# A chunked linear-attention kernel: transpositions of the decays traced at the end of a group's preparation, and 32x32 merge products that alternate two heads

## The chip, the cores and the metric

The kernel runs on one core of a Trainium2 chip. The metric is the device time of one execution in microseconds (us), and the time given for a kernel is the median of its runs. Five engines work beside each other, each through its own queue in order: TensorE (PE, with its weight loads shown apart as PEld), VectorE (DVE), ScalarE (ACT), GpSimd (POOL) and SyncE (SP), which issues the transfers here.

## The reference

A recurrent attention over 768 steps for 4 x 8 heads of 40 elements, and behind it a gated network and a chain of plain products, all in fp32. The change lies in the first part:

```python
def _attn_ref(r, k, v, w, a, b):
    B, H, S, D = r.shape            # 4, 8, 768, 40
    state = np.zeros((B, H, D, D), dtype=np.float32)
    y = np.zeros_like(r)
    for t in range(S):
        ...
        y[:, :, t] = np.einsum('bhd,bhde->bhe', rt, state)
        Sa = np.einsum('bhde,bhe->bhd', state, at)
        state_decay = state * wt[:, :, None, :] - np.einsum('bhd,bhe->bhde', Sa, bt)
        state = state_decay + np.einsum('bhd,bhe->bhde', vt, kt)
    return y
...
x = attn_out.transpose(0, 2, 1, 3).reshape(B * S, H * D)
h = x @ moe_w_in                    # 320 -> 2048
x = (h * (1.0 / (1.0 + np.exp(-h)))) @ moe_w_out
h = (x @ moe2_w1) * (x @ moe2_w2) @ moe2_w3
out = h @ moe2_w_out
```

## The kernel before

The 768 steps are cut into 12 chunks of 64, and two chunks make a group, so there are 6 groups. The 32 heads are handled as 16 pairs: the even head of a pair lies on partitions 0 to 63, the odd one on 64 to 127 (`par`, with `q = 64 * par`).

**Preparation (`prep`, once for each group).** The group's w, b, k, a and r are loaded. VectorE multiplies w up step by step into running products (F forwards, G backwards), which scale b, k and a; the results go to DRAM (Bd, Kd, Ad, Fd, Rd) and come back in the layout of the chunks (X, Abd, Rbd). On the way `FCn` gets each chunk's total decay (L164, and a second copy by ScalarE, L166), and `decay` turns it round: TensorE transposes FCn into PSUM (`pt`, L219) and ScalarE copies it into `FC[g]` (L222). FC[g] multiplies the state in the chain when chunks 2g and 2g + 1 are about to be entered (L450, L453). `check` (L765, L766) tests on ScalarE whether w stays in bounds, and overwrites w.

**A (`A`, `A_out`, once for each chunk).** X is transposed (L264) and multiplied with Abd (L272) into a triangular matrix A2, of which `A_out` hands the diagonal 32x32 blocks (Lc) and the block below them (L21) on.

**Inverse and merge.** `invp` and `inverse` invert the 32x32 diagonal blocks of two chunks by elimination, on GpSimd from group 2 on (31 steps of two operations, L341 and L345, into T), and VectorE transposes T into TD (L356). Then `merge`, once for each chunk: VectorE transposes TD into TW (L379); the first product p1 (L385) multiplies L21 with TW, ScalarE copies it in two halves over TW (L387); the second product p2 (L398) multiplies TW with TD, and ScalarE copies it into TT (L400). Each product has 16 matmuls of 32x32 for the even heads and 16 for the odd ones. In p1 head q has its operands on partitions q to q + 31 and its result on q + 32 to q + 63; in p2 it is the other way round. `busy` puts a few idle matmuls ahead of a product (L372).

**Chain.** Four blocks of four pairs for each chunk go through `pp` (L415), `pu` (L436), `pz` (L444, L445), `pv` (L458), `pg` (L464) and `py` (L473, L475), with copies by ScalarE (Pb L419, UV L438 and L454, VT L460) and VectorE (UV L437, Z L452 and L453, GT L466, x L478) between them. Then the network (`moe`, hp L659 and yp L689) runs over all tokens.

**What sets the order.** Up to the first merge the order on SP, PE, ScalarE and VectorE is the order of the program text (`manual_schedule`). After it, steps of preparation, A, inverse and merge are tasks with due times between the steps of the chain, and a scheduler orders every engine's instructions by its own simulated time line; what is traced earlier goes first where it can. The queues then run in that fixed order.

Of the kernel before, what the change touches and what calls it, by code (L numbers as in the profile page):

```python
# [19 lines left out]
NP = B * H // 2  # L20
DP = 104  # L21
# [3 lines left out]
class Kernel:  # L25
# [73 lines left out]
    def prep(s, g, first=False):  # L99
# [3 lines left out]
        nc, V, ACT = s.nc, s.nc.vector, s.nc.scalar  # L103
# [4 lines left out]
        def load(n):  # L108
            t = s.bt(early.get(n, "in"), [128, 32, 40], "in_")
            for u in range(2):  # L110
                for c in range(2):
                    q = 64 * u + 32 * c
                    s.ld(out=fl(t)[q : q + 32], in_=s.lanes(n, g)[u, c])
            return t
# [15 lines left out]
        def store_t(out, o):  # L130
            for c in range(2 if first else 1):
                for u in range(2):
                    l, n = 32 * c, 32 if first else 64
                    d = dict(out=out[l : l + n, :, 32 * u : 32 * u + 32], in_=o[64 * u + l : 64 * u + l + n])
                    rest.append(d) if c else s.ld(**d)
# [25 lines left out]
            mul(FI[:, i + 1, 7], FI[:, i + 1, 7], FI[:, i, 7])  # L161

        ACT.copy(GI[0:64, 3, 7], F[64:128, 32])
        P = s.FCn[:, 0:40]  # L164
        mul(P, F[:, 32], GI[:, 3, 7])
        ACT.copy(s.FCn[:, 64:104], P)  # L166
        for i in (2, 1, 0):
            mul(GI[:, i, 7], GI[:, i, 7], GI[:, i + 1, 7])
        V.reciprocal(F[:, 0], P)
        s.decay(g)  # L170
        yield 800
        mul(GI[:, :, 0:7], GI[:, :, 0:7], GI[:, :, 7:8].to_broadcast([128, 4, 7, 40]), nc.gpsimd if s.GPP[min(g, 2)] else V)
        yield 1400
# [11 lines left out]
        f = eight(F[:, 0:32])  # L185
# [17 lines left out]
        r = load("r")  # L203
# [2 lines left out]
        o = s.bt("o", [128, 40, 32], "o")  # L206
        ACT.copy(o, r.rearrange("p t e -> p e t"))
        store_t(s.Rd[g], o)
        yield 0

    def after(s):
# [3 lines left out]
    def decay(s, g):  # L215

        nc = s.nc
        pt = s.PS([128, 128], "pt")
        nc.tensor.transpose(pt[0:DP, :], s.FCn, s.idn)  # L219
        for par in range(2):  # L220
            q = 64 * par
            nc.scalar.copy(s.FC[g][q : q + 40], pt[q : q + 40, 0:64].rearrange("p (c r a) -> p c r a", c=2, a=2)[:, :, :, par])  # L222
# [152 lines left out]
    def merge(s, c):  # L375

        nc, TT, TD, L21 = s.nc, s.TT[c // 2 % 2][:, c % 2], s.TD[:, c % 2], s.L21[c % 3]
        TW = s.sm0.tile([128, NP, 32], F32, name="TW")
        nc.vector.transpose(out=TW, in_=TD)  # L379
        p1 = s.PS([128, NP, 32], "p1")  # L380
        s.busy(p1, s.MD[0] if c > 1 else 0)
        for par in range(2):
            q = 64 * par
            for r in range(NP):
                nc.tensor.matmul(p1[q + 32 : q + 64, r], lhsT=L21[q : q + 32, r], rhs=TW[q : q + 32, r], start=True, stop=True)  # L385
        for q in (0, 64):
            nc.scalar.copy(TW[q + 32 : q + 64], p1[q + 32 : q + 64])  # L387
        e = s.copies(c, "T")
        for i in range(4):
            q, o = slice(32 * i, 32 * i + 32), 32 * (i % 2)  # L390
            e[i % len(e)](TT[q, :, o : o + 32], TD[q])
        yield 1200
        p2 = s.PS([128, NP, 32], "p2")
        s.busy(p2, s.MD[1] if c > 1 else s.MD[2])
        for par in range(2):
            q = 64 * par
            for r in range(NP):
                nc.tensor.matmul(p2[q : q + 32, r], lhsT=TW[q + 32 : q + 64, r], rhs=TD[q + 32 : q + 64, r], start=True, stop=True)  # L398
        for q in (0, 64):
            nc.scalar.copy(TT[q : q + 32, :, 32:64], p2[q : q + 32])  # L400
        yield 1200
# [513 lines left out]
    def run(s):  # L915
        nc = s.nc
        with ExitStack() as ctx:
# [10 lines left out]
            for half in range(2):  # L928
                q = msk[64 * half : 64 * half + 64]
# [1 line left out]
            s.mskb = msk.unsqueeze(1).to_broadcast([128, 8, 64])  # L931
            att = ctx.enter_context(ExitStack())
            s.sm0 = att.enter_context(s.tc.tile_pool(name="sm0", bufs=1))
            s.FCn = s.zeros(s.sm0, "FCn", [128, DP], eng="act")
            s.FC = [s.zeros(s.sm0, f"FC{g}", [DP, 2, NP], eng="act") for g in range(6)]

            def drain(gen):
# [165 lines left out]
            act, n = [], 0  # L1103
# [55 lines left out]
```

## Time and profile before

| | |
|---|---|
| median of 3 runs | 1330.17 us (1322.04 to 1330.79) |
| profiled execution | 1328.77 us, its span 1327.1 us |
| TensorE busy | 1166.2 us, 88% of the span |
| VectorE, ScalarE, GpSimd busy | 698.6, 525.3, 304.8 us |
| merge products, first and second | 33.4 and 35.9 us of TensorE |

The times of the table's lower rows are busy times of one profiled execution; engines overlap, so they do not add up. Roughly, the first 92 us are loading and preparation of the first groups, up to 640 us the attention runs, and from there the network. A row of a time line gives the start in us from the beginning of the span, the time until the last of its instructions ended, the engine, the line, what is written and read, and in brackets the idle time before it with what ended that.

### The profile page before, as it was taken

The numbers are of one execution on the slowest core, as the hardware profiler recorded it, in microseconds if no ns is written. First come the engines' busy times: TensorE is split into PE (matmuls) and PEld (weight loads), VectorE is DVE, ScalarE is ACT, GpSimd is POOL, SyncE is SP. The second block draws the span as 40 slices with busy tenths as digits, with TensorE's granted clock in tenths as the row PEclk, the third lists the DMA queues.
The fourth block names the chain that finished last, engine by engine and source line by source line (L and its number), as shares of the span: only waits on it lengthen the run. The fifth ranks groups of instructions, "written<-read, shape, count | busy, mean of one in ns | idle before, by whom it ended". The sixth has DMA issues, their size and how long they took to land. (4 is left out here: it accounts for less than half of the span.)

```text
span 1327.1 us, 26016 instructions
## 1 busy us (share of the span) xinstructions
PE 1166.2 (88%) x10416; PEld 1029.0 (78%) x10416; DVE 698.6 (53%) x1358; ACT 525.3 (40%) x1155; POOL 304.8 (23%) x540
## 2 busy tenths in 40 slices
PE   3876979959847999899876899999999999999996
PEld 1666878859747889898765788889889889988985
DVE  7687771593585566648999414324424423433331
ACT  4546344434435445346455323323323323332321
POOL 4143400630811834702555320000000000000000
PEclk9885665876967889989887899999999999999998
DMA  9959885476667552747312001001001001000000
GB/s 213 192 103 204 139 173 90 87 158 100 127 172 148 104 122 71 214 130 199 114 45 70 1 12 29 1 0 41 1 1 40 0 1 35 6 0 20 1 1 23
DMA packets 258273, 105.86 MB, mean 80 GB/s; under 512 B 226400, under 2 KB 246880, under 8 KB 258144
## 3 DMA queue, kind: packets, MB, share of 16 engines
q1 hardware_dynamic: 258144, 104.12, 35.7%
q8 instruction: 84, 1.38, 0.5%
q14 instruction: 45, 0.37, 0.1%
HBM read 75.24 MB, written 28.84 MB: 78 GB/s over the span
## 5 line engine op out<-in xcount | busy, mean ns | idle before, releaser
L659 PE MATMUL hp<-xH,w 128*128 128x512 f32 x704 | 249.7, 398 | 4.8 <-ACT xH L488 4.2
L689 PE MATMUL yp<-w,gH 128*128 128x320 f32 x1152 | 231.9, 317 | 15.1 <-ACT gH L488 15.1
L689 PEld LDWEIGHTS yp<-w,gH 128*128 128x128 f32 x1152 | 194.1, 194 | 29.1 <-ACT gH L488 19.2
L667 DVE TENSOR_TENSOR sg<-sg,hp 128x512 f32<-128x512 f32 x144 | 99.0, 687 | 219.5 <-ACT sg L666 199.7
L489 DVE TENSOR_TENSOR gL<-sg,gH 128x512 fp32r<-128x512 f32 x120 | 82.9, 691 | 148.4 <-ACT gH L488 93.2
L659 PEld LDWEIGHTS hp<-xH,w 128*128 128x128 f32 x704 | 131.8, 189 | 31.3 <-ACT xH L488 5.6
L488 ACT CAST gH<-sg 128x512 fp32r<-128x512 f32 x144 | 89.3, 620 | 163.2 <-PE yp L689 87.4
L689 PE MATMUL yp<-w,gL 128*128 128x320 f32 x576 | 143.7, 313 | 0.1
L659 PE MATMUL hp<-xL,w 128*128 128x512 f32 x352 | 139.3, 396 | 0.0
L689 PEld LDWEIGHTS yp<-w,gL 128*128 128x128 f32 x576 | 101.8, 191 | 2.9 <-POOL gL L489 0.4
L666 ACT ACTIVATE sg<-hp 128x512 f32<-128x512 f32 x96 | 57.3, 597 | 107.8 <-PE hp L659 90.1
L345 POOL TENSOR_TENSOR T<-T,tmp 128x87 f32<-128x87 f32 (+31 forms) x186 | 96.1, 517 | 14.5
L341 POOL TENSOR_TENSOR tmp<-T,L 128x87 f32<-128x87 f32 (+31 forms) x186 | 89.3, 480 | 41.3 <-DVE L L324 26.9
L659 PEld LDWEIGHTS hp<-xL,w 128*128 128x128 f32 x352 | 66.4, 189 | 11.6
L666 ACT COPY sg<-hp 128x512 f32<-128x512 f32 x48 | 28.2, 587 | 107.1 <-DVE gL L489 48.4
L272 PE MATMUL pl<-Abd,XT 104*128 104x128 f32 x384 | 60.2, 311 | 10.8 <-ACT XT L266 10.8
L659 PE MATMUL hp<-xA,w 128*128 128x512 f32 x176 | 69.4, 394 | 0.0
L659 PE MATMUL hp<-xB,w 128*128 128x512 f32 x176 | 67.3, 394 | 0.0
L273 DVE TENSOR_TENSOR A<-pl,msk 128x512 f32<-128x512 f32 x48 | 33.1, 690 | 59.8 <-PE pl L272 59.7
L272 PEld LDWEIGHTS pl<-Abd,XT 104*128 104x128 f32 x384 | 54.3, 220 | 13.0 <-ACT XT L266 10.4
L604 POOL COPY row<-row 128x64 f32<-128x64 f32 x20 | 5.5, 274 | 255.4 <-DMA row<-xd 254.5
L473 PE MATMUL py<-Xt,GT 128*64 128x40 f32 x768 | 58.9, 261 | 4.8 <-DVE GT L466 4.8
(249 smaller groups left out, 2168.3 us busy)
## 6 DMA issues: line engine op xcount, KB each, us to landing
w3q<-in_moe_w_dram SPq DMA_DIRECT2D x16, 512.0 KB
wq<-in_moe_w_out_dram SPq DMA_DIRECT2D x24, 320.0 KB
wq<-in_moe_w_in_dram SPq DMA_DIRECT2D x16, 256.0 KB
wq<-in_moe_w_dram SPq DMA_DIRECT2D x16, 256.0 KB
Xt<-Bd SPq DMA_DIRECT2D x24, 160.0 KB
Xt<-Kd SPq DMA_DIRECT2D x24, 160.0 KB
Abd<-Ad SPq DMA_DIRECT2D x48, 80.0 KB
Fd<-F SPq DMA_DIRECT2D x12, 320.0 KB
```

Of the source, the lines that this page charges most:

```text
L272: nc.tensor.matmul(pl[:, hp], lhsT=XT[b][:, hp], rhs=Abd[b // 2][0:DP, 4 * (b % 2) + hp], start=True, stop=True)
L273: nc.vector.tensor_tensor(out=A2[:, 4 * b : 4 * b + 4, :].rearrange("p h (a t) -> p (h a) t", a=2), in0=pl.rearrange("p h (a t) -> p (h a) ...
L341: e.tensor_tensor(out=t3, in0=T[:, a:b, j : j + 1].to_broadcast([128, n, m]), in1=L[:, j : j + 1, j + 1 : 32].to_broadcast([128, n, m]), o ...
L345: s.last = e.tensor_tensor(out=T[:, a:b, j + 1 : 32], in0=T[:, a:b, j + 1 : 32], in1=t3, op=ALU.add)
L473: s.pe = nc.tensor.matmul(py[q : q + 64, 4 * bb + hp], lhsT=GT[:, hp, q : q + 64], rhs=X[:, r0 + hp, q : q + 40], start=True, stop=(c == 0))
L488: s.nc.scalar.copy(hi, raw)
L489: (eng or s.nc.vector).tensor_tensor(out=lo, in0=raw, in1=hi, op=ALU.subtract)
L604: s.nc.gpsimd.tensor_copy(r[:, 320:384], r[:, 256:320])
L659: nc.tensor.matmul(p, lhsT=a, rhs=b, start=j == 0, stop=j == 7)
L666: nc.scalar.activation(out=sg, in_=p, func=func) if func else nc.scalar.copy(sg, p)
L667: nc.vector.tensor_tensor(out=sg, in0=sg, in1=q, op=ALU.mult)
L689: nc.tensor.matmul(y, lhsT=a[:, sl], rhs=W[:, b], start=first and j == 0, stop=last and j == 2)
```

## The change

The call of `decay(g)` moves from the middle of a group's preparation to its very end, behind the store of r; so that the next group does not overwrite FCn meanwhile, there are two FCn, used in turn. In both products of the merge the loop over the heads goes inside the loop over the pairs, so that matmuls of the even and of the odd head take turns.

```diff
+        FCn = s.FCn[g % 2]
+        P = FCn[:, 0:40]
         mul(P, F[:, 32], GI[:, 3, 7])
-        ACT.copy(s.FCn[:, 64:104], P)
+        ACT.copy(FCn[:, 64:104], P)
         for i in (2, 1, 0):
             mul(GI[:, i, 7], GI[:, i, 7], GI[:, i + 1, 7])
         V.reciprocal(F[:, 0], P)
-        s.decay(g)
         yield 800
...
         store_t(s.Rd[g], o)
+        s.decay(g)
         yield 0
...
-        nc.tensor.transpose(pt[0:DP, :], s.FCn, s.idn)
+        nc.tensor.transpose(pt[0:DP, :], s.FCn[g % 2], s.idn)
...
-        for par in range(2):
-            q = 64 * par
-            for r in range(NP):
+        for r in range(NP):
+            for q in (0, 64):
                 nc.tensor.matmul(p1[q + 32 : q + 64, r], lhsT=L21[q : q + 32, r], rhs=TW[q : q + 32, r], start=True, stop=True)
...
-        for par in range(2):
-            q = 64 * par
-            for r in range(NP):
+        for r in range(NP):
+            for q in (0, 64):
                 nc.tensor.matmul(p2[q : q + 32, r], lhsT=TW[q + 32 : q + 64, r], rhs=TD[q + 32 : q + 64, r], start=True, stop=True)
...
-            s.FCn = s.zeros(s.sm0, "FCn", [128, DP], eng="act")
+            s.FCn = [s.zeros(s.sm0, f"FCn{i}", [128, DP], eng="act") for i in range(2)]
```

Line numbers after the call of `decay` shift by one. The scheduler's order changes with it at some places; three of them follow.

TensorE in chunk 5, before: the transposition of group 5 stands between two pairs of `pg` products.

```order
L458 MATMUL pv<-idn,UVb_607 104x128 x4
L464 MATMUL pg<-Rbd_223,VT 128x128 x8
L219 MATMUL pt<-idn,FCn 104x128
L464 MATMUL pg<-Rbd_225,VT 128x128 x8
L372 MATMUL p_4035<-idn 128x128 x2
```

The same place in the program now (`pg` is L463):

```order
L457 MATMUL pv<-idn,UVb_601 104x128 x4
L463 MATMUL pg<-Rbd_225,VT 128x128 x8
L463 MATMUL pg<-Rbd_227,VT 128x128 x8
L373 MATMUL p_4033<-idn 128x128 x2
```

The transposition is gone from there; it now stands behind the last `pu` of chunk 6. Those of groups 3 and 4 moved in the same way from chunks 1 and 3 to chunks 2 and 4, those of groups 0 and 1 from the start of the program to the first merge.

VectorE at the end of group 5's running products, before: FCn, then the preparation and conversions of weights (wr), then chunk 6's TD, Lc and TW.

```order
L106 TENSOR_TENSOR F<-F 128x40 x3
L106 TENSOR_TENSOR FCn<-F,G 128x40
...
L106 TENSOR_TENSOR G<-G 128x4x280
L499 SCALAR_TENSOR_TENSOR wr<-wq_4240,wr 128x320
L356 STREAM_TRANSPOSE TD<-T 128x32x32
L191 SCALAR_TENSOR_TENSOR o<-in__4177,F 128x1280
L106 TENSOR_TENSOR in__3863<-in__3863,G 128x1280
L106 TENSOR_TENSOR in__4130<-in__4130,G 128x1280
L292 COPY Lc<-A_3643 32x16x32 x4
L379 STREAM_TRANSPOSE TW<-TD 128x512
```

The same engine and place now:

```order
L357 STREAM_TRANSPOSE TD<-T 128x32x32
L106 TENSOR_TENSOR G<-in__3849,G 128x3x40
L106 TENSOR_TENSOR F<-F 128x40
L293 COPY Lc<-A_3645 32x16x32 x4
L380 STREAM_TRANSPOSE TW<-TD 128x512
L106 TENSOR_TENSOR F<-F 128x40
...
L465 TENSOR_TENSOR GT<-pg,msk 128x512
L477 TENSOR_TENSOR x<-py,Fn 128x320
L106 TENSOR_TENSOR F<-F 128x40
...
L106 TENSOR_TENSOR FCn_150<-F,G 128x40
```

TD, Lc and TW of chunk 6, and two GT, moved ahead of FCn and of what follows it.

TensorE at the merge of chunk 0, before: the first product, the second, the first `pp` of the chain.

```order
L385 MATMUL p_856<-TW,L_217 32x32 x32
L398 MATMUL p_895<-TD,TW 32x32 x32
L415 MATMUL pp<-UV_601,A_361 64x40 x8
```

The same place now:

```order
L220 MATMUL pt<-idn,FCn_148 104x128
L385 MATMUL p_854<-TW,L_219 32x32 x32
L397 MATMUL p_893<-TD,TW 32x32
L414 MATMUL pp<-UV_595,A_355 64x40 x8
L397 MATMUL p_893<-TD,TW 32x32 x31
```

The `pp` moved in between the first matmul of the second product and its other 31, of which the next one is of the other head. Second products are split so in all merges but that of chunk 4. (The rows don't tell the heads apart.)

## Rows read from the trace of the kernel before

**Rows 1.** The page's head.

```profile
span 1327.1 us, 26016 instructions
```

**Rows 2.** Windows: stretch, length, busy time of PE, PEld, DVE, ACT, POOL, clock, DMA.

```profile
92.00:640.00 548.00, 466.97 (x6794) 426.10 (x6794) 339.31 (x691) 249.49 (x606) 194.02 (x350) 0.78 0.65 140
640.00:1327.00 687.00, 642.91 (x3372) 563.96 (x3372) 291.50 (x479) 231.03 (x472) 77.47 (x107) 0.96 0.07 19
```

**Rows 3.** Time line of PE: transpositions of groups 3 to 5, and chunk 6's merge.

```profile
181.97 0.46 PE L219 MATMUL pt<-idn,FCn 128*104 128x128 f32 x1 [7.08 <-DMA Abd<-Ad]
...
281.79 0.46 PE L219 MATMUL pt<-idn,FCn 128*104 128x128 f32 x1 [11.88 <-ACT FCn L166]
...
375.00 0.45 PE L219 MATMUL pt<-idn,FCn 128*104 128x128 f32 x1 [13.25 <-ACT FCn L166]
...
388.36 3.43 PE L385 MATMUL p<-TW,L 32*32 32x32 f32 x64 [6.41 <-DVE TW L379]
```

**Rows 4.** Time line of ACT ahead of group 3's transposition.

```profile
178.10 0.58 ACT L460 COPY VT<-pv 104x512 f32<-104x512 f32 x1
178.72 1.36 ACT L765 ACTIVATE in__1599<-in__1599,small 128x1280 f32<-128x1280 f32 x1
...
181.71 0.21 ACT L166 COPY FCn<-FCn 128x40 f32<-128x40 f32 x1
```

**Rows 5.** Merge products: time lines of PE and ACT, then groups (busy, mean ns).

```profile
92.72 3.40 PE L385 MATMUL p<-TW,L 32*32 32x32 f32 x64 [5.52 <-DVE TW L379]
...
96.15 1.18 ACT L387 COPY TW<-p 32x512 f32<-32x512 f32 x2 [3.05 <-PE p L385]
...
96.78 3.43 PE L398 MATMUL p<-TD,TW 32*32 32x32 f32 x64 [0.67 <-ACT TW L387]
...
314.32 2.11 PE L385 MATMUL p<-TW,L 32*32 32x32 f32 x64
...
L398 PE MATMUL p<-TD,TW 32*32 32x32 f32 x768 | 35.9, 222 | 8.1 <-ACT TW L387 8.1
L385 PE MATMUL p<-TW,L 32*32 32x32 f32 x768 | 33.4, 215 | 13.4 <-DVE TW L379 13.3
```

**Rows 6.** Windows of 10 ns, L385 on PE alone: passes in flight (x), clock.

```profile
93.90:93.91 0.01, 0.01 (x5) 0.50 0.61 112
94.40:94.41 0.01, 0.01 (x8) 0.50 0.37 68
...
314.80:314.81 0.01, 0.01 (x6) 1.00 0.89 141
315.40:315.41 0.01, 0.01 (x9) 1.00 0.84 128
```

**Rows 7.** Time line of ACT in group 0's preparation.

```profile
11.06 0.22 ACT L163 COPY G<-F 64x40 f32<-64x40 f32 x1 [0.94 <-DVE F L106]
```

**Rows 8.** Time line of DVE after group 4's running products.

```profile
280.18 0.20 DVE L106 TENSOR_TENSOR FCn<-F,G 128x40 f32<-128x40 f32 x1 [1.03 <-ACT G L163]
...
291.20 0.69 DVE L466 TENSOR_TENSOR GT<-pg,msk 128x512 f32<-128x512 f32 x1
...
294.32 0.71 DVE L379 STREAM_TRANSPOSE TW<-TD 128x512 f32<-128x512 f32 x1
```

**Rows 9.** Time lines of POOL and DVE ahead of chunk 6's merge.

```profile
371.58 0.30 POOL L345 TENSOR_TENSOR T<-T,tmp 128x31 f32<-128x31 f32 x1
...
377.87 2.08 DVE L356 STREAM_TRANSPOSE TD<-T 128x1024 f32<-128x1024 f32 x1
...
385.16 2.41 DVE L292 COPY Lc<-A 32x512 f32<-32x512 f32 x4
...
387.60 0.71 DVE L379 STREAM_TRANSPOSE TW<-TD 128x512 f32<-128x512 f32 x1
```

**Rows 10.** Time lines of POOL in chunk 8's inverse, of DVE after chunk 10's.

```profile
454.99 0.94 POOL L489 TENSOR_TENSOR wo<-wr,wo 128x320 fp32r<-128x320 f32 x1 [3.26 <-ACT wo L488]
...
558.69 2.16 DVE L356 STREAM_TRANSPOSE TD<-T 128x1024 f32<-128x1024 f32 x1 [0.66 <-POOL T L345]
```

More of the change, by code (lines that the diff above doesn't have):

```diff
@@ L163, in prep @@
         ACT.copy(GI[0:64, 3, 7], F[64:128, 32])
-        P = s.FCn[:, 0:40]
+        FCn = s.FCn[g % 2]
+        P = FCn[:, 0:40]
         mul(P, F[:, 32], GI[:, 3, 7])
-        ACT.copy(s.FCn[:, 64:104], P)
+        ACT.copy(FCn[:, 64:104], P)
         for i in (2, 1, 0):
```

## The prediction

> **What bounds the kernel now.** I read the page first, then the windows by stage, then the TensorE timeline for its idle time. The profiled execution took 1328.77 us, of which 1327.1 us are the span [rows 1]; the median of the three runs, 1330.17, is 1.4 us above that execution, against which I sum. From 640 us on TensorE is busy 642.9 of 687 us at a mean granted clock of 0.96 [rows 2]: this is the gated network, which the change does not touch. From 92 to 640 us, the attention stage, TensorE is busy 467.0 of 548 us at a mean clock of 0.78, while VectorE has 339.3 and ScalarE 249.5 us [rows 2]. TensorE is the engine with the least slack there, and its queue holds everything in one order, so a microsecond of it saved or of idling removed counts, unless another wait stands right behind.
>
> What does it idle on? Three waits stand out: each time the transposition of a group's decays (`pt`, L219), 7.08, 11.88 and 13.25 us, 32.2 us in all [rows 3]. Two are released by ScalarE's copy into FCn (L166). The first is put down to a DMA, but it starts at 181.97, 0.05 us after that copy ended at 181.92 [rows 3, 4], so it is the same wait. The transposition stands in TensorE's queue between the second and the third `pg` product of a chunk; everything behind it waits, though nothing there needs FC yet: group g's FC is first used by chunk 2g - 1, and group 3's transposition stands in chunk 1.
>
> The other target is the merge: 12 merges of two products, each of 32 small matmuls, which the trace splits into 64 passes. One such product takes 3.43 us at the 1.2 GHz level and 2.11 us at 2.4 GHz [rows 5]. All 24 keep TensorE busy 35.9 + 33.4 = 69.3 us [rows 5]; n x 3.43 + (24 - n) x 2.11 = 69.3 gives n = 14 at the low level and 10 at the high one.
>
> **The change, part by part.**
>
> *The alternation.* Passes of one head follow each other at 3.43/64 = 53 ns at 1.2 GHz and 2.11/64 = 33 ns at 2.4 GHz. Both heads' tiles are disjoint (rows and columns at 0 and 64). No product of before alternates, but each contains one change from head to head in its middle, and there the trace shows what two heads do together: the passes in flight in a 10 ns window go from 5 to 8 in a product at the low level and from 6 to 9 in one at the high level [rows 6]. So the heads run side by side. Bounds: no gain, or half the time, that is 14 x 1.71 + 10 x 1.05 = 34 us of TensorE time. I take the half, since the counts at the change are nearest to it.
>
> On the other side, the page "TensorEngine Tiling (Array Packing)" of the Trainium skill (Restrictions and Gotchas, Gotcha 1) says that different row tiles cannot access one PSUM bank simultaneously; both heads write the one tile p1. The rise from 5 to 8 in flight speaks against it here. By that rule this term would be zero or worse; it is the last rival below.
>
> The alternation has one cost: the second product reads TW, which ScalarE copies in two halves, 1.18 us for both, from 96.15; the product begins at 96.78, after the first half [rows 5]. Now its second matmul needs the second half: 1.18/2 = 0.59 us later. In 11 of 12 merges the scheduler has put other matmuls into that hole (shown with the change for chunk 0), so it costs between 0 and 0.6 us; I charge 0.6.
>
> *The transposition.* Its two instructions, one matmul and two ScalarE copies per group, remain; the three waits go, the pipeline behind them is what counts. The second FCn costs one zeroing copy on ScalarE at the start, hidden by the 0.94 us that ScalarE waits for VectorE a little later [rows 7]. Groups 0 and 1 move behind the warm-up matmuls, where FCn is long ready: nothing. What is late next, stall by stall:
>
> - Group 3 (175 to 182). ScalarE now has the check of w (L765, 1.36 us, and L766) ahead of the last `VT` copies, which ended at 178.68 before [rows 4]. So `pg` is held until about 181 to 183 anyway; the wait mostly changes its name. The gain is the transposition's 0.5 us, both products of chunk 2 (1.7 + 1.1), and VectorE's third GT, freed earlier: 6 us, bounds 2 and 8.
> - Group 4 (270 to 282). Before, VectorE's third GT stood behind 11 us of preparation (FCn at 280.18, GT at 291.20); now it comes right behind FCn. TensorE runs `pg`, `py` and the next chunk's `pp` in the hole, but chunk 4's first product still needs TW, which began at 294.32 before [rows 8] and now comes about 1.5 us later, since another GT of 0.69 us and two smaller operations moved ahead of it. So about 6 of 11.88 us come back at once as a wait at the merge; 6 us stay, bounds 2 and 9.
> - Group 5 (362 to 388). Here the order on VectorE changes most (shown with the change): TD, Lc and TW of chunk 6's merge now stand before FCn. TD needs GpSimd's last T, ready at 371.88; TD 2.08, Lc 2.41 and TW 0.71, with 0.6 us of multiplications between, make TW ready at about 377.7 instead of 388.31 [rows 9]. The merge, which waited 6.41 us more behind the stall [rows 3], starts 10.6 us earlier and is 1.7 us shorter: 12 us, bounds 4 (if the order's gain is lost at GpSimd) and 15.
>
> Sum of the three: 24 us. Products outside these stretches give half their time (1.7 us at the low level, 1.05 at the high one), less 0.6 for each second one. Chunk 3, both low: 1.7 + 1.1. Chunk 5, high and low: 1.05 + 1.1. Chunk 7, both high: 1.05 + 0.45. Together 6.4. Chunks 8 to 11, seven of eight high: 4 x 1.05 + 3 x 0.45 + 1.1 = 6.6, of which I keep 3, because there the inverse on GpSimd binds: VectorE's TD of chunks 10 and 11 waited 0.66 us for GpSimd's last T [rows 10], so what TensorE gains ahead of it is partly waited for. Chunks 0 and 1: nothing, since the first `pp` now stands inside the merge and ScalarE's queue sets the second one. Against: GpSimd has four splits `wo` inside chunk 8's inverse where it had two, and one of them waited 3.26 us [rows 10]: 1.5 us. Sum: 24 + 6.4 + 3 - 1.5 = 32 us. 1328.8 - 32 = **1297**.
>
> The clock is not in the sum. Less idling may lift the mean of 0.78, shorter products may lower it; 467 us x 0.78/0.80 = 455 is an estimate from [rows 2] of what 0.02 is worth: some 10 us either way.
>
> **The rivals.**
>
> *Everything pays:* the stalls go whole and the products halve: 32.2 + 34 = 66 us, 1263. Against it: in groups 4 and 5 the merge waits for VectorE's TW [rows 3, 8, 9], which no transposition holds up. Half-way, 1280, is as far as I believe it.
>
> *The waits only change their names:* FCn is late because the preparation is, and the same preparation feeds ScalarE's VT and VectorE's TW. Then the three stalls return at `pg` and at the merges, and the products leave 13 us: 1316. For it: groups 3 and 4 above. Against: group 5, where TW itself moves ahead.
>
> *The alternation doesn't do what it says:* passes stay at 53 and 33 ns, and only the stalls pay: 24 less their products' share of 6, less the 6 us of second copies, 12 us: 1317.
>
> *Slower:* each change of tile waits until the last matmul has left. A pass takes 215 to 222 ns from start to end on average [rows 5] instead of a pace of 53 or 33, so a change would cost some 0.17 us; 30 new ones make 5 us a product, 120 us for 24, less the stalls' 18: 1430. The point from which it decides: 18 us / 24 / 30 = 25 ns a change. Against it: at the change of head the count in flight rises [rows 6], where this would let it fall to 1. It is what the rule of the Trainium skill's page above, "TensorEngine Tiling (Array Packing)", would make of the kernel.
>
> **How the numbers follow.** The forecast, 1285 to 1312 with its bounds and the clock: 0.62. Everything pays, 1263 to 1284: 0.14. New names, 1310 to 1325: 0.14. No alternation: 0.06. Slower: 0.04. The range that leaves a tenth out on either side is 1275 to 1319. A measurement here tells 1% (13 us) from no change, so faster needs less than 1317: the forecast, the first rival, half of the second and a third of the third make 0.85; slower 0.04; the same 0.11.
>
> **What would show it.** In the profile after: products of 1.8 and 1.2 us in place of 3.43 and 2.11, with about twice as many passes in flight; no TensorE idle time in front of `pt`; in its place waits of `pg` on VT near group 3, and of chunk 4's merge on TW of some 6 us; chunk 6's merge following its TD by some 6 us, ahead of FCn; an unchanged stretch after attention, which starts some 32 us earlier. The prediction is wrong if the scheduler's new order makes a wait that none of these rows shows, above all on GpSimd's inverse in the second half, or if the mean clock of the attention stage moves by more than 0.02.

## The result and the profile after

The changed kernel takes 1311.09 us (median of 20 runs, 1301.77 to 1320.89) against 1326.36 of the kernel before (20 runs in turn with it): a ratio of 0.988, 95% interval 0.9859 to 0.9901, or 15.9 us less, with 2.8 either way. The forecast was 32 less. The profiled execution took 1312.28 us, 1310.6 of them the span, which is 16.5 less than [rows 1].

The windows of the changed kernel by stage (stretch, length, busy time of PE, PEld, DVE, ACT, POOL, clock, DMA):

```profile
92.00:640.00 548.00, 450.43 (x6866) 405.44 (x6867) 349.19 (x720) 257.76 (x631) 211.16 (x361) 0.80 0.66 144
640.00:1310.60 670.60, 627.23 (x3303) 548.63 (x3301) 273.94 (x450) 221.96 (x449) 67.29 (x97) 0.97 0.06 16
```

The attention stage's mean clock is 0.80 against 0.78 [rows 2], just at the bound that the prediction set. TensorE's busy time up to 640 us fell by 16.5 us although more of the program lies there now.

**The products.** The time line of TensorE:

```profile
93.00 1.92 PE L385 MATMUL p<-TW,L 32*32 32x32 f32 x64 [5.40 <-DVE TW L380]
95.59 0.31 PE L397 MATMUL p<-TD,TW 32*32 32x32 f32 x2 [0.68 <-ACT TW L387]
95.83 1.08 PE L414 MATMUL pp<-UV,A 128*64 128x40 f32 x16
96.84 1.91 PE L397 MATMUL p<-TD,TW 32*32 32x32 f32 x62
...
316.53 1.20 PE L385 MATMUL p<-TW,L 32*32 32x32 f32 x64
```

The groups of the two lines (busy, mean ns of a pass, idle time ahead of them):

```profile
L397 PE MATMUL p<-TD,TW 32*32 32x32 f32 x768 | 23.5, 222 | 19.8 <-ACT TW L387 19.8
L385 PE MATMUL p<-TW,L 32*32 32x32 f32 x768 | 18.0, 210 | 18.9 <-DVE TW L380 18.9
```

Windows of 10 ns on L385 alone (passes in flight in brackets, clock behind them):

```profile
94.60:94.61 0.01, 0.01 (x9) 0.50 0.71 170
...
317.00:317.01 0.01, 0.01 (x12) 1.00 1.21 512
```

A product takes 1.92 us at the low level and 1.20 at the high one instead of 3.43 and 2.11 [rows 5], with 9 and 12 passes in flight instead of 5 and 6 [rows 6]: the two heads run side by side, as forecast. A pass alone still takes 210 to 222 ns. The second product has the hole behind its first matmul (two passes), filled with `pp`. All 24 cost 41.5 us instead of 69.3, 27.8 less. But the idle time ahead of them rose from 21.5 us [rows 5] to 38.7, 17.2 us more, as waits for TW. That need not be the price of alternating: the two experiments below that have the moved transposition and r's copy on GpSimd wait 33.1 us there without alternation (e9) and 34.8 with it in 22 products (e6).

**The waits.** The time line of TensorE where it waited, in order (what released it in brackets):

```profile
156.03 1.92 PE L265 MATMUL px<-idn,Xt 128*104 128x128 f32 x8 [3.89 <-DMA Xt<-Kd]
...
176.38 3.75 PE L273 MATMUL pl<-Abd,XT 104*128 104x128 f32 x16 [8.03 <-DVE G L106]
...
190.72 1.16 PE L463 MATMUL pg<-Rbd,VT 104*128 104x128 f32 x8 [3.24 <-ACT VT L459]
...
303.32 0.91 PE L385 MATMUL p<-TW,L 32*32 32x32 f32 x26 [8.69 <-DVE TW L380]
...
380.76 1.20 PE L385 MATMUL p<-TW,L 32*32 32x32 f32 x64 [1.56 <-DVE TW L380]
```

No idle time stands in front of `pt` any more. The wait of `pg` for VT near group 3 (3.2 us), that of chunk 4's merge for TW (8.7 us), and the earlier merge of chunk 6, 7.6 us ahead of [rows 3], are those that the prediction named. The first two rows are new, and no row of the prediction spoke of them. All that TensorE waited for VT ahead of `pg` between 92 and 640 us, before and in the changed kernel (us in total, times, the longest):

```profile
PE pg L464 <- ACT VT L460: 6.3, 5, 3.1
PE pg L463 <- ACT VT L459: 24.4, 9, 7.7
```

So 18.1 us more are waited for at `pg` and 17.2 us more at the merges, in place of the 32.2 us at `pt`.

VectorE at chunk 6's merge has the forecast order, TW behind TD by 4.8 us instead of 9.7 [rows 9], and FCn behind both:

```profile
375.23 2.06 DVE L357 STREAM_TRANSPOSE TD<-T 128x1024 f32<-128x1024 f32 x1
377.47 2.49 DVE L293 COPY Lc<-A 32x512 f32<-32x512 f32 x4
379.99 0.71 DVE L380 STREAM_TRANSPOSE TW<-TD 128x512 f32<-128x512 f32 x1
386.96 0.19 DVE L106 TENSOR_TENSOR FCn<-F,G 128x40 f32<-128x40 f32 x1
```

**Busy time, idle time and the clock.** Windows from 92 us to the end of the last merge (columns as above): the kernel before, the changed one, and e2 and e9 of the experiments, which have the moved transposition and no alternation:

```profile
92.00:594.16 502.16, 424.44 (x6149) 388.94 (x6149) 301.26 (x596) 222.44 (x524) 181.53 (x334) 0.76 0.64 135
92.00:572.79 480.79, 389.34 (x6157) 351.70 (x6159) 297.61 (x597) 222.16 (x526) 187.58 (x334) 0.79 0.66 141
92.00:578.79 486.79, 397.52 (x6150) 363.55 (x6150) 297.20 (x597) 222.83 (x526) 183.71 (x334) 0.82 0.67 140
92.00:569.83 477.83, 399.13 (x6150) 365.50 (x6150) 298.71 (x597) 219.96 (x525) 186.15 (x335) 0.82 0.68 143
```

In the changed kernel this stretch is 21.4 us shorter. TensorE is busy 35.1 us less in it, but its idle time (length less busy time) rose from 77.7 to 91.5 us. In e2, which runs the same products head after head, the busy time fell by 26.9 us and the idle time rose by 11.6; in e9 the busy time fell by 25.3 and the idle time rose by 1.0 (its execution lies 9 us above its median, of which more at the end). What differs for the matmuls there is the granted clock, 0.82 on average instead of 0.76. It shows most from the second product of chunk 1 to the first of chunk 3, the kernel before and then e2:

```profile
110.50:210.50 100.00, 84.08 (x1039) 76.46 (x1039) 70.12 (x166) 40.62 (x100) 24.67 (x64) 0.62 0.81 160
111.60:197.30 85.70, 68.73 (x1038) 62.57 (x1038) 67.68 (x161) 41.52 (x103) 24.79 (x64) 0.79 0.83 160
```

So in these traces the gain of the moved transposition is not idle time removed; it is TensorE running a larger share of its time at the 2.4 GHz level. The other executions agree: the mean clock of a whole execution is 0.905 to 0.913 in the six of e2, and 0.884 to 0.900 in the 18 of the kernel before beside them. Why the level rose is not shown by any run.

**Where the time came from.** Once per pair of chunks VectorE transposes Lc into L, which starts the pair's inverse: a good mark. The kernel before, then the changed one, time line of VectorE:

```profile
238.27 1.93 DVE L324 STREAM_TRANSPOSE L<-Lc 128x1024 f32<-128x1024 f32 x1
...
330.17 1.98 DVE L324 STREAM_TRANSPOSE L<-Lc 128x1024 f32<-128x1024 f32 x1
...
428.66 1.90 DVE L324 STREAM_TRANSPOSE L<-Lc 128x1024 f32<-128x1024 f32 x1
```

```profile
245.05 1.93 DVE L325 STREAM_TRANSPOSE L<-Lc 128x1024 f32<-128x1024 f32 x1
...
332.63 1.94 DVE L325 STREAM_TRANSPOSE L<-Lc 128x1024 f32<-128x1024 f32 x1
...
416.75 1.98 DVE L325 STREAM_TRANSPOSE L<-Lc 128x1024 f32<-128x1024 f32 x1
```

The last merge ends at 594.16 us before and at 572.79 after. The forecast's terms, put into the same stretches (a chunk's products go where its merge stands):

| stretch | terms of the forecast | forecast | measured |
|---|---|---|---|
| up to L of chunks 4 and 5 | group 3 stall, chunk 3's products | -8.8 | +6.8 |
| to L of chunks 6 and 7 | group 4 stall, chunk 5's products | -8.2 | -4.3 |
| to L of chunks 8 and 9 | group 5 stall, chunk 7's products | -13.5 | -14.4 |
| to the end of the last merge | chunks 8 to 11, less `wo` | -1.5 | -9.5 |
| behind it | nothing | 0 | +4.9 |
| sum | | -32 | -16.5 |

So the shortfall is the first stretch: 15.6 us worse than forecast. The rest nearly balances, the last two rows by misses of 8.0 and 4.9 us in opposite directions. These are stretches of one execution of each kernel, and a stretch can agree with the forecast where its terms do not, as the part on the prediction shows.

### The profile page after: what moved, and what is told of

Same layout as the page of the kernel before. It is cut to its first block, busy times and chain, and to the rows that moved or that the text cites. A ratio compares the mean times of both kernels' runs of the same rounds, so it can differ in the third digit from the quotient of the medians.

```text
span 1310.6 us, 26013 instructions
## 1 busy us (share of the span) xinstructions
PE 1133.8 (87%) x10416; PEld 992.8 (76%) x10416; DVE 690.8 (53%) x1358; ACT 524.1 (40%) x1156; POOL 311.7 (24%) x540
## 5 line engine op out<-in xcount | busy, mean ns | idle before, releaser
L688 PE MATMUL yp<-w,gH 128*128 128x320 f32 x1152 | 228.7, 314 | 12.8 <-ACT gH L487 12.7
L688 PEld LDWEIGHTS yp<-w,gH 128*128 128x128 f32 x1152 | 190.8, 191 | 26.9 <-ACT gH L487 16.9
L342 POOL TENSOR_TENSOR tmp<-T,L 128x87 f32<-128x87 f32 (+31 forms) x186 | 96.1, 517 | 41.3 <-DVE L L325 27.2
L346 POOL TENSOR_TENSOR T<-T,tmp 128x87 f32<-128x87 f32 (+31 forms) x186 | 95.3, 512 | 14.4
L273 PE MATMUL pl<-Abd,XT 104*128 104x128 f32 x384 | 65.8, 329 | 22.7 <-ACT XT L267 13.2
L273 PEld LDWEIGHTS pl<-Abd,XT 104*128 104x128 f32 x384 | 59.1, 236 | 25.7 <-ACT XT L267 13.0
L463 PE MATMUL pg<-Rbd,VT 104*128 104x128 f32 x384 | 55.0, 300 | 24.4 <-ACT VT L459 24.4
L463 PEld LDWEIGHTS pg<-Rbd,VT 104*128 104x128 f32 x384 | 51.0, 212 | 26.6 <-ACT VT L459 26.4
L658 PE MATMUL hp<-xA,w 128*128 128x512 f32 x176 | 69.3, 396 | 0.0
```

The lines of the kernel that those rows point to most:

```text
L273: nc.tensor.matmul(pl[:, hp], lhsT=XT[b][:, hp], rhs=Abd[b // 2][0:DP, 4 * (b % 2) + hp], start=True, stop=True)
L342: e.tensor_tensor(out=t3, in0=T[:, a:b, j : j + 1].to_broadcast([128, n, m]), in1=L[:, j : j + 1, j + 1 : 32].to_broadcast([128, n, m]), o ...
L346: s.last = e.tensor_tensor(out=T[:, a:b, j + 1 : 32], in0=T[:, a:b, j + 1 : 32], in1=t3, op=ALU.add)
L463: s.pe = nc.tensor.matmul(pg[:, hp], lhsT=VT[:, hp], rhs=Rbd[:, 4 * bb + hp], start=True, stop=True)
L658: nc.tensor.matmul(p, lhsT=a, rhs=b, start=j == 0, stop=j == 7)
L688: nc.tensor.matmul(y, lhsT=a[:, sl], rhs=W[:, b], start=first and j == 0, stop=last and j == 2)
```

## The experiments

Each was timed in 5 rounds against the kernel before; us are the ratio's distance from 1 times 1326. e1 to e4, e5 to e8 and e9 to e12 ran on three chips, each with the kernel before beside it, so runs are compared by these ratios. The profiled executions of the runs with the first product head after head (1321.16 us), and of the moved transposition alone with r on GpSimd (1303.3), lie 9 us above their medians, and that of e10 (1309.5) 7 us, so what is read from these three is the order of things, single waits, and sums of busy time and of waits.

| run | median us | ratio (95%) | us |
|---|---|---|---|
| e1 alternation alone | 1323.16 | 0.9963 (0.9945 to 0.9981) | -4.9 |
| e2 transposition alone | 1311.34 | 0.9888 (0.9855 to 0.9920) | -14.9 |
| e3 changed, second product from chunk 2 on | 1309.72 | 0.9867 (0.9839 to 0.9895) | -17.6 |
| e4 second product of chunks 0, 1 alone | 1336.42 | 1.0080 (1.0051 to 1.0110) | +10.6 |
| e5 first products, transposition from group 2 on | 1304.99 | 0.9868 (0.9829 to 0.9907) | -17.5 |
| e6 e3, r on GpSimd | 1293.88 | 0.9768 (0.9739 to 0.9797) | -30.8 |
| e7 e3, preparation due later | 1291.98 | 0.9749 (0.9726 to 0.9772) | -33.3 |
| e8 changed, first product head after head | 1311.71 | 0.9888 (0.9865 to 0.9912) | -14.9 |
| e9 e2, r on GpSimd | 1294.10 | 0.9777 (0.9741 to 0.9813) | -29.6 |
| e10 changed, r on GpSimd | 1302.49 | 0.9827 (0.9798 to 0.9857) | -22.9 |
| e11 before, r on GpSimd | 1324.73 | 0.9999 (0.9974 to 1.0024) | -0.1 |
| e12 e5, r on GpSimd | 1294.12 | 0.9782 (0.9741 to 0.9823) | -28.9 |

### The parts, and the queue of loads

The first theory (A) was that the lost first stretch comes from the queue of loads. The changed kernel's queue, time line of SP (all of Abd between 140 and 175 us):

```profile
147.43 0.52 SPq L51 DMA_DIRECT2D Abd<-Ad  x1
...
155.13 0.53 SPq L51 DMA_DIRECT2D Abd<-Ad  x1
...
164.54 2.01 SPq L51 DMA_DIRECT2D in__1601<-in_w_dram  x4
...
170.08 1.51 SPq L51 DMA_DIRECT2D Abd<-Ad  x2
```

In the kernel before all four stand in a row, ahead of the load of w:

```profile
144.01 2.20 SPq L51 DMA_DIRECT2D Abd<-Ad  x4
```

Half of Abd for chunk 4 is issued 26 us later, behind the load of w and those of chunk 5's Xt, and `pl` waits for it at 176 us. The profile of the changed kernel puts that wait down to VectorE; the same wait in e10, whose queue has the same order, shows the transfer:

```profile
175.94 3.33 PE L273 MATMUL pl<-Abd,XT 104*128 104x128 f32 x14 [7.89 <-DMA Abd<-Ad]
```

**e1**, the alternation alone:

```diff
-        for par in range(2):
-            q = 64 * par
-            for r in range(NP):
+        for r in range(NP):
+            for q in (0, 64):
                 nc.tensor.matmul(p1[q + 32 : q + 64, r], ...
```

and the same for p2.

> The kernel before with both merge products alternating and the transposition of the decays left where it was. Theory A (the change loses some 9 us between 92 and 200 us, because the second product of chunks 0 and 1, alternated, changes the order of the load queue, and gains about 25 us after that): the three waits at pt stay, the products save some 34 us of TensorE time of which about a third counts, and the 9 us are lost, so -5 against the kernel before, between -10 and +2. Rival B (the queue of loads is not the cause; the waits of groups 3 and 4 came back in full under other names): the products pay alone, -12 to -15.

Measured -4.9 us: as A has it, and not B's -12 to -15.

**e2**, the transposition alone; against the changed kernel, for p1 and p2:

```diff
-        for r in range(NP):
-            for q in (0, 64):
+        for par in range(2):
+            q = 64 * par
+            for r in range(NP):
```

> The kernel before with the transposition of the decays moved to the end of the preparation, and the products head after head as they were. Theory A: the order of the queue of loads up to 180 us stays nearly that of before, so nothing is lost there, and the stalls pay 18 us without their products' share: -18 against the kernel before, between -12 and -24. Rival B: the waits come back under other names and only group 5 pays: -2 to -10.

Measured -14.9 us, between the two ranges' centres and inside A's. The moved transposition gives by itself all that the whole change gives.

**e3**, the changed kernel with one loop changed:

```diff
-        for r in range(NP):
-            for q in (0, 64):
+        for r, q in [(r, q) for r in range(NP) for q in (0, 64)] if c > 1 else [(r, q) for q in (0, 64) for r in range(NP)]:
                 nc.tensor.matmul(p2[q : q + 32, r], ...
```

> The changed kernel, but the second product of chunks 0 and 1 is head after head as before. Theory A: the second half of Abd for chunk 3 is loaded before the loads of group 2 again, the waits of 3.9 and 8.0 us for Xt and Abd at 156 and 176 us go, and the kernel is 9 to 14 us faster than the changed one: -25 to -30 against the kernel before, near the forecast. Rival B: two products of 24 are 1.5 us each slower, so +1 to +3 against the changed kernel, -13 to -15 against the one before.

(Chunk 3 and group 2 in this text should read chunk 4 and group 3.) Measured -17.6 us: A's -25 to -30 failed, and B's -13 to -15 lies within the interval. **e4** is its opposite, against the kernel before:

```diff
-        for par in range(2):
-            q = 64 * par
-            for r in range(NP):
+        for r, q in [(r, q) for r in range(NP) for q in (0, 64)] if c < 2 else [(r, q) for q in (0, 64) for r in range(NP)]:
                 nc.tensor.matmul(p2[q : q + 32, r], ...
```

> The kernel before with only the second product of chunks 0 and 1 alternating. Theory A: the queue of loads gets the order of the changed kernel, and the kernel is 5 to 12 us slower than the one before, the loss lying ahead of 200 us. Rival B: nothing but two shorter products: -3 to +1.

Measured +10.6 us: A is right that this edit, with the order that it sets, costs some 10 us. That it does so through the late loads is read from the traces; no run moves the loads alone. Then why does e3 not gain it? Its trace has a new wait. Time lines of SP, ScalarE and TensorE in e3:

```profile
186.12 1.30 SPq L51 DMA_DIRECT2D in__2265<-in_r_dram  x3
...
208.36 0.62 SPq L51 DMA_DIRECT2D in__2265<-in_r_dram  x1
...
211.18 2.67 ACT L207 COPY o<-in__2265 128x1280 f32<-128x1280 f32 x1 [14.43 <-DMA in__2265<-in_r_dram]
...
215.26 1.07 ACT L267 COPY XT<-px 104x512 f32<-104x512 f32 x2
...
215.89 1.01 PE L273 MATMUL pl<-Abd,XT 104*128 104x128 f32 x3 [16.09 <-ACT XT L267]
```

ScalarE's copy of group 3's r into o waits 14.4 us, because the last of the four parts of r is issued at 208 us, 21 us behind the other three, with stores and other loads between. The XT copy is queued behind it on ScalarE, and TensorE waits 16.1 us for XT. (The Trainium skill's page "Perfetto Trace Analysis", section Tensor Engine Instruction, says that ScalarE's execution queue is a strict FIFO; these rows agree.) The copy waits 5.2 us in the kernel before, 5.25 in the changed one and 12.0 in e2.

### The copy of r, and the order on VectorE

Theory C: this wait, and VectorE's order at chunk 6's merge, hold what the forecast promised. Rival D: the chain of pairs takes everything back.

**e5**, the changed kernel with e2's edit for p2 alone, and:

```diff
         V.reciprocal(F[:, 0], P)
+        if g < 2:
+            s.decay(g)
...
         store_t(s.Rd[g], o)
-        s.decay(g)
+        if g > 1:
+            s.decay(g)
```

> The changed kernel with the second products head after head in all chunks and the transposition of groups 0 and 1 at its old place. The load queue then has the second half of Abd early, and on VectorE TD, Lc and TW of chunk 6's merge stand before FCn of group 5, as in the changed kernel. Theory C (the forecast's gain in group 5 rides on that order on VectorE, which the run with the second product alternated from chunk 2 on had lost): chunk 6's first product starts within 7 us of the end of GpSimd's inverse instead of 20, and the time is 1299 to 1304. Rival D (the pairs' chain through GpSimd's inverse takes back whatever is gained ahead of it, whatever VectorE's order): 1308 to 1312.

The order came as meant. e3 has TW 10.5 us behind TD; e5 has 4.7 (VectorE and TensorE, e3 first):

```profile
366.11 2.08 DVE L357 STREAM_TRANSPOSE TD<-T 128x1024 f32<-128x1024 f32 x1
376.65 0.71 DVE L380 STREAM_TRANSPOSE TW<-TD 128x512 f32<-128x512 f32 x1
...
377.42 0.80 PE L385 MATMUL p<-TW,L 32*32 32x32 f32 x22 [9.63 <-DVE TW L380]
```

```profile
364.68 2.03 DVE L360 STREAM_TRANSPOSE TD<-T 128x1024 f32<-128x1024 f32 x1
369.42 0.71 DVE L383 STREAM_TRANSPOSE TW<-TD 128x512 f32<-128x512 f32 x1
370.18 1.00 PE L388 MATMUL p<-TW,L 32*32 32x32 f32 x51 [0.63 <-DVE TW L383]
```

But the ratio, 0.9868, is that of e3, 0.9867, and its interval reaches over D's range and into C's: inconclusive by itself.

**e6**, e3 with one line changed:

```diff
-        ACT.copy(o, r.rearrange("p t e -> p e t"))
+        nc.gpsimd.tensor_copy(o, r.rearrange("p t e -> p e t")) if g == 3 else ACT.copy(o, r.rearrange("p t e -> p e t"))
```

> The run with the second product alternated from chunk 2 on, with one edit: the copy of group 3's r into o is made by GpSimd instead of ScalarE; all queues keep their order. Theory C: ScalarE's wait of 14.4 us for the fourth part of r (at 197 to 211 us) is what TensorE waits for at pl, 16.1 us, and it goes: the next pair's L is ready 8 to 13 us earlier and the time is 1298 to 1304. Rival D: the 16 us are waited for at the next merge or for GpSimd, and the time stays at 1308 to 1311.

Measured -30.8 us, 13.1 (with 5.3 either way) less than e3: C, and rather more than it foretold. Time lines of TensorE and GpSimd:

```profile
201.00 1.16 PE L273 MATMUL pl<-Abd,XT 104*128 104x128 f32 x8
...
212.86 2.67 POOL L207 COPY o<-in__2265 128x1280 f32<-128x1280 f32 x1 [62.10 <-ACT A L317]
```

The copy still comes at 213 us, but on an engine that had been idle for 62 us, and `pl` runs at 201 us, without a wait.

**e7**, e3 with the due time of the preparation moved:

```diff
-    PX, PA, PI, PT, PM, PP1, PP2, PW, NACT = 0.0, 0.05, 0.6, 0.2, 0.8, 0.1, -0.2, 6.0, 4
+    PX, PA, PI, PT, PM, PP1, PP2, PW, NACT = 0.0, 0.05, 0.6, 0.2, 0.8, 0.1, 0.0, 6.0, 4
```

> The run with the second product alternated from chunk 2 on, with the preparation due 0.2 of a chunk later, which has all four parts of r ahead of the stores in the queue of loads and TD, Lc and TW of chunk 6's merge ahead of FCn of group 5. Theory C: both holes go, 16 us at pl and 10 us at chunk 6's merge, of which the chain of pairs returns some: 1288 to 1300. Rival D: 1306 to 1311.

Measured -33.3 us, within C's range. In this kernel chunk 8's Xt is loaded from 329.2 us on, behind its transposition, which starts at 319.5 and so takes the tile as chunk 3 left it; a wait for that load is missing from the time. With two edits in one and this gap, it supports e6 and shows nothing of its own.

**e8**, the changed kernel with e2's edit for p1 alone; every queue keeps its order:

> The changed kernel with the first product of every merge head after head as before; every engine and queue keeps the changed kernel's order, so this prices the first product's alternation alone. Twelve products, 1.51 us longer at the low level and 0.91 at the high one, are some 14 us of TensorE time. Theory C (the first product stands in the chain from GpSimd's inverse over TD and TW to the next pair, so most of it counts): +7 to +12 against the changed kernel. Rival D (TensorE waits on the chain and shorter products are waited for at the next step): +0 to +4.

It is 1.1 us slower than the changed kernel, with 4.2 either way: D. The twelve first products have 13.1 us more TensorE time in all (31.1 against 18.0), of which at most some 5 reach the end. Ahead of the products TensorE waits 34.1 us in e8 and 38.7 in the changed kernel, so 4.6 of the 13.1 stand there.

### What is worth what

**e9**, e2 with the line of e6:

> The kernel with only the transposition moved, and group 3's copy of r into o on GpSimd instead of ScalarE. Theory E (what the change gains ahead of 200 us is waited for at ScalarE's copy of r, whose load stands late in the queue of loads, and TensorE behind ScalarE): ScalarE's wait of 12.0 us at this copy goes, and the time falls from 1311 to 1297 to 1302; what is then left to the run with alternation and the same edit, at 1294, is what alternating is worth, 3 to 8 us. Rival F (the run with alternation and this edit was faster for the alternation): 1306 to 1311.

**e10**, the changed kernel with it:

> The changed kernel with group 3's copy of r on GpSimd, all queues in their order. Here ScalarE waits 5.25 us at this copy and TensorE 3.9 us behind it at chunk 3's second product. Theory E: -2 to -5 against the changed kernel, 1306 to 1309, since this kernel has lost its time before, at the loads of Xt and Abd. Rival F (taking 2.7 us of copying off ScalarE is a gain of its own): -12 to -16, as in the run with the second product alternated from chunk 2 on.

**e11**, the kernel before with it:

> The kernel before with group 3's copy of r on GpSimd, nothing else. ScalarE waits 5.2 us at this copy, TensorE 1.5 us behind it. Theory E: 0 to -3 against the kernel before. Rival F: -12 to -16, and then the gain of this edit has nothing to do with the change.

**e12**, e5 with it:

> The run with the first products alone alternating and the transposition moved from group 2 on, with group 3's copy of r on GpSimd. It has both the early load of Abd and chunk 6's merge ahead of FCn on VectorE. Theory E: the wait of 15.3 us at pl (203 to 218 us) goes, and the time falls from 1305 to 1288 to 1294, below the run at 1294. Rival D (the pairs' chain takes it back at the next merges): 1299 to 1305.

e11 measured -0.1 us: the edit alone is worth nothing, and rival F falls. e9 measured -29.6, 14.7 less than e2 (6.4 either way): E, and a little more than its range; the 3 to 8 us that E left to alternation are not found. e9 and e6 differ by 1.2 us (6.1 either way): with 22 of 24 products alternating the kernel is no faster than with none, within that (the second product's loop changes the order of the queues too, so the two differ in more than the alternation). e10 is 7.0 us below the changed kernel (4.8 either way): more than E's 2 to 5 and less than F's 12 to 16, with E's range nearly all in the interval and F's just outside; it stays 7.8 us above e6 (5.5 either way), which is the loss of e4 again. e12, at 1294.12, is at the edge of E's range and below D's; but it isn't below e6 (1.9 us above it, 6.7 either way), although chunk 6's merge starts at 356.9 us in it and at 364.1 in e6. In the two traces this lead is 1.5 us at the next L (396.0 and 397.5) and gone at the one behind it (475.2 and 474.3), as rival D has it; the two kernels differ in the second products as well, so that it is the chain that takes the lead back is not shown.

e6, e9 and e12, all at 1294 us, beat both kernels. The simplest is e9: the transposition at the end and r's copy on GpSimd, without any alternation.

## Why the prediction had the direction and twice the gain

The change is faster, and 1311 lies in the range, 1 us inside its upper end. But the sum was twice the gain, and the gain has another form than the sum: it took the three stalls for TensorE time won, and in the trace the waits stand elsewhere, while TensorE's busy time fell. That 1311 lies in the range is in part luck: the clock, which the sum left out, gave back some of what the waits took.

From the runs, edit by edit: the moved transposition with r's copy on GpSimd gives -29.6 (e9); the alternation of 22 products 1.2 more (e6); the alternated second product of chunks 0 and 1 takes 7.8 (e10 against e6; e4 alone 10.6); r's copy back on ScalarE takes 7.0 (the changed kernel against e10). That is -16.0, and -15.9 was measured, as it must be, since each step starts where the last one ended. On another path a step has another price: r's copy is worth 14.7 between e2 and e9. By the prediction's steps:

- *"Chunks 0 and 1: nothing."* This step failed. The prediction looked at the ScalarE wait there and not at the queue of loads, whose order the alternated second product changes: Abd for chunk 4 is issued 26 us later. Cost 8 to 11 us (e4, e10 against e6), with all else that this edit's order changes.
- *Group 3, 6 us.* The prediction said that this wait mostly changes its name, and it does. What it missed is the clock. From the second product of chunk 1 to the first of chunk 3 (shown with the clock above) e2 needs 14.3 us less than the kernel before, with 17.0 us of idle time instead of 15.9: its whole lead is busy time, at a mean granted clock of 0.79 instead of 0.62. ScalarE's wait for r, which none of the prediction's rows showed, then takes most of it back (e2 against e9, e3 against e6). In the changed kernel the step above hides the lead.
- *The products' half.* The time of a product is right within 0.2 us. (The two heads' tiles are disjoint, as the prediction says, but not both by rows and columns at 0 and 64: in the first product the rows are at 0 and 64 and the columns at 32 and 96, in the second the other way round.) The term is not: 6.4 + 3 us, and a share of the stalls, were booked for it, and the runs leave 1 us for the first products (e8, at most some 5) and 1 us for 22 products (e9 against e6, at most some 7). Where the rest went is not settled: the waits ahead of the products take 4.6 of the 13.1 us in e8, and are about the same in e9 and e6. With the transposition in its old place the same 22 products are worth 15.5 us (4.6 either way, e1 against e4; their orders differ too, and their mean clocks up to the last merge, 0.81 and 0.77), so the two parts of the change don't add. Why they don't is not settled by a run.
- *Groups 4 and 5, 6 and 12 us.* In the changed kernel both stretches came within 4 us. Group 4's stall does return, and whole: 7.7 us at `pg` (280 us) and 8.7 at the merge, where the prediction let 6 us come back. Of group 5's 13.2 us and the 6.4 at the merge behind it, 6.1 are left at `pg` (372.5 us) and 1.6 at the merge: 12 less, as forecast. That this comes from VectorE's new order holds at that merge, but e12 against e6 shows that a kernel without this order there reaches the same end.
- *The clock, left out of the sum.* The prediction estimated 0.02 of the mean clock at "some 10 us either way". Up to the last merge it rose by 0.03 in the changed kernel and by 0.06 in e2, where 26.9 us of busy time went with the same matmuls. Whether the stalls' going, the new order of the queues or something else raised it, no run tells.
- *The rest unchanged.* Of 21.4 us at the last merge 16.5 are left at the end. VectorE is busy 64.8 of 70 us between 650 and 720, as before (65.2); whether its conversion of weights binds there was not tried.
- *The rivals.* "Everything pays" fails for the products, and for the stalls too: e9's 29.6 us are near to its 32.2, but e9's idle time is that of the kernel before. "New names" comes nearest in number to 1311 with its 1316, and is right on the waits, which did come at `pg` and the merges (18.1 and 17.2 us more) and at loads besides; it has the gain as the products' alone, where e2 has nearly all of it without them. The other two, no alternation and slower, fall with the products' 1.92 and 1.20 us. By the rule of the Trainium skill's page "TensorEngine Tiling (Array Packing)", Gotcha 1, that different row tiles cannot access one PSUM bank simultaneously, the products would not have become shorter; here both heads write one PSUM tile in turn, and 64 passes take 1.20 us instead of 2.11.

## What to carry to other kernels

A stall removed is worth what the next thing in each in-order queue allows: list, for the stretch behind it, what stands at the head of ScalarE's queue and what of its inputs is still to be issued in the queue of loads. Where a scheduler sets the orders, an edit to TensorE can move a load by 26 us on another queue, so read the load queue's new order before booking "nothing" for an edit. Do not book TensorE time saved at its full length: 13.1 us of it were worth 1.1 (4.2 either way) in e8. And when an edit removes stalls, compare busy time, idle time and the granted clock of the stretch before and after: here the stalls' idle time came back under other names, and the gain stood in the busy time.

## What was not expected of the hardware

Passes of two 32x32 tiles, alternating, into one PSUM tile keep 12 in flight at the 2.4 GHz level; 64 take 1.20 us, 19 ns each, the last one's 0.2 us of flight included. And executions of one kernel spread over 19 us (1301.77 to 1320.89 of the changed kernel), so that a single trace can lie 9 us from its median, and a term of a few us needs the runs. The mean clock of the whole execution goes with it, 0.912 in the fastest and 0.890 in the slowest of the changed kernel; and in the trace of e9, 9 us above its median, TensorE has a granted clock of 0.50 from 180 to 200 us, where that of e2 has 0.86.
